# Constant tiles in another order, and what begins at a multiple of 128 bytes

## The chip, the core and the metric

The kernel runs on one core of a Trainium2 chip. The metric is the device time of one execution in microseconds; lower is better. Of several executions the median stands.

## What is computed

Three stages follow each other: a chunked scan with a decay, then a gated layer (SiLU), then a layer with a squared ReLU. All inputs of the layers' weights arrive as 64-bit floats.

```python
def _attn_ref(x, a, B, C):            # x: (4, 8, 768, 32); B, C: (4, 8, 768, 16)
    for c in range(nc):               # chunks of 32 steps
        L = np.exp(cum[:, :, :, None] - cum[:, :, None, :]) * causal
        M = np.einsum('bhin,bhjn->bhij', Cc, Bc) * L
        y[:, :, sl] = M @ xc + np.einsum('bhin,bhnd->bhid', Cc, state) * np.exp(cum)[..., None]
        state = ...                   # decayed state + sum of B x
...
x = attn_out.transpose(0, 2, 1, 3).reshape(3072, 256)
g = x @ w_gate                        # 256 x 1536
x = (g / (1 + np.exp(-g)) * (x @ w_val)) @ w_out      # 1536 x 256
h = np.maximum(x @ w_in, 0)           # 256 x 2048
out = (h * h) @ w_out                 # 2048 x 256
```

## The kernel before

**Stages.** The scan is cut into 28 chunks of 112 (the last of a batch element 96) steps, 7 for each of 4 batch elements. Chunk k has its x in one of three tiles xa, B and C in one of three tiles bc (late chunks) or two tiles eb (early ones), and its decay matrix in one of two tiles mt. Its output goes, transposed, to two large constant tiles: xh_all and xl_all hold the scan's output (and later the gated layer's) as a high and a low part, so that a product of 32-bit numbers is done as three fast matmuls: high by high, high by low, low by high. Weights are turned to 32-bit numbers on the chip (raw, then v) and split into hi and lo, each a tile of 1024 numbers per partition.

**Matmuls.** In the gated layer (function `glu`) the tokens are cut into tiles of 336, 432, 256 and four times 512. For each tile and each of 12 blocks of 128 columns, `front` makes g and v, each from six matmuls (L743) with hi or lo as the stationary and xh_all or xl_all as the moving operand. ACT and DVE make the product t of the two, and from it the tile p with a high and a low half. `back` adds to two accumulators with six matmuls (L857), whose moving operand is p. In the second layer (function `relu2`) six tiles of 512 tokens run over 16 blocks: six matmuls for h (L743), relu on ACT (L909), square on DVE (L912), high half on ACT (L915), low half on DVE (L919), and six matmuls (L929) with p as the moving operand. In the last of the six tiles p is the stationary operand and the matmuls are 256 wide (L938). Order on PE within a six: high weights by high, high weights by low, low weights by high; then the same for the second half.

**Order.** All work is recorded as operations with a cost and a priority, and the class `Graph` plans the order once, from a table of numbers (`PLAN`). The order of instructions on each engine is that of the plan.

**Addresses.** Tiles are laid out in a partition one after another in the order in which they are made, each rounded up to a multiple of 32 bytes: first a few constants, then the tiles of the pool `const`, then the pools w (weights), raw, tmp (t), p, tr, L, ab, xf, st. The tiles of the pools have sizes that are multiples of 128 bytes. So the place where w begins, and with it every later tile, follows from the sum of the sizes of the constant tiles. xh_all and xl_all are the first of them.

Of `const`, two tiles have a size that is no multiple of 128 and not small: delta (1808 bytes in a partition) and dv (3164). spare holds one number, which `act_table` writes to have the table of functions loaded early.

Of the kernel before, what the change touches and what calls it, by code (L numbers as in the profile page):

```python
# [8 lines left out]
F32 = mybir.dt.float32  # L9
F32R = mybir.dt.float32r  # L10
F16 = mybir.dt.float16
BF16 = mybir.dt.bfloat16
# [3 lines left out]
AF = mybir.ActivationFunctionType  # L16
# [117 lines left out]
def kernel(  # L134
# [13 lines left out]
    nc = tc.nc  # L148
    NB, H, S, D = x.shape
# [8 lines left out]
    P = 128  # L158
    G = P // D
    HG = H // G  # L160
    Q = P - NS
# [17 lines left out]
    const = ctx.enter_context(tc.tile_pool(name="const", bufs=1))  # L179
# [8 lines left out]
    NBC, NX, NEB, NMT = 3, 3, 2, 2  # L188
# [6 lines left out]

    xh_all = const.tile([P, 2, T], F32R, name="xh_all")
    xl_all = const.tile([P, 2, T], F32R, name="xl_all")
    delta = const.tile([P, H, Q + 1], BF16, name="delta")
    bc = [const.tile([P, 2, H, NS], F32, name=f"bc{i}") for i in range(NBC)]
    eb = [const.tile([P, 4, P], F32, name=f"eb{i}") for i in range(NEB)]  # L200
    xa = [const.tile([P, H, D], F32, name=f"xa{i}") for i in range(NX)]
    mts = [const.tile([P, H, P], F32, name=f"mt{i}") for i in range(NMT)]
    idle = const.tile([P, 256], BF16, name="idle")
    eye = const.tile([P, P], F32, name="eye")
    pick = const.tile([P, H], F32, name="pick")
    spare = const.tile([1, 1], F32, name="spare")
    dv_all = const.tile([P, NCB, Q + 1], F32, name="dv")
    dv = dv_all[0:R]
    C0 = PLAN["parts"]
# [24 lines left out]

    def act_table():

        nc.scalar.activation(spare, nc.const_aps.tensor(0.0, (1, 1), F32), AF.Silu)


    def zeros():  # L240
# [79 lines left out]
    op_delta = g.add("POOL", 1250, setup_delta, [op_mt], prio=-996)  # L320
    op_bc = g.add("POOL", 2200, setup_bc, prio=-900)
    op_tab = g.add("ACT", 600, act_table, prio=-940)

    def dma(eng, n, cost, move, fn, deps=(), prio=0.0, bufs=(), pieces=256):
# [797 lines left out]
    spare=0,  # L1122
# [107 lines left out]
```

## Time and profile before

| | us |
|---|---|
| median of 3 runs | 642.64 |
| lowest, highest | 641.45, 644.4 |
| the profiled execution | 640.49 |
| its span, first to last instruction | 638.7 |

The span has 9952 instructions. The page gives, for each engine, busy time and its share; a chain of work that ended last; and groups of instructions by line. The names to know: PE does matmuls, PEld loads their stationary operands and overlaps PE, DVE and ACT work on elements, POOL does some of the chunks' steps, SP issues nearly all transfers. A matmul's own duration in the records runs from its start to its modelled end and overlaps with the next one; the distance between two starts is what one costs in a stream. Starts stand in the timeline, in hundredths of a microsecond from the span's start, so a distance is best read over many matmuls. In the timeline equal neighbours are merged into one row with a count.

The run has four parts. Up to some 45 us transfers of weights and chunks set the pace and PE fills gaps with idle matmuls; up to 145 us PE does the chunks and the gated layer for tiles of 336, 432 and 256; up to 362 us the gated layer for tiles of 512, with the small matmuls of 15 chunks in between; then the second layer, the last tile of it from 594 us.

### The profile page before, as it was taken

Reading aid. Unit: us, or ns where it says so; the run is one execution under the profiler, and the core shown is the slowest. Engines: PE = TensorE matmul, PEld = TensorE weight load, DVE = VectorE, ACT = ScalarE, POOL = GpSimd, SP = SyncE. Lnnn points to the kernel's source line nnn. Section 1 sums busy time; section 2 is a strip of 40 time slices with the busy share of each in tenths; the row PEclk is TensorE's granted clock in tenths of the full one; section 3 lists DMA queues with packets and bytes.
Section 4 is the critical chain, followed back from the end, with each engine's and each line's share of the span. In section 5 each row is a group of like instructions: output and inputs, shape, how many; then the busy total and the mean of one; then the engine's idle time right before and its main releaser. Section 6 shows DMA issues by size and latency. Waiting matters only on the chain.

```text
span 638.7 us, 9952 instructions
## 1 busy us (share of the span) xinstructions
PE 631.1 (99%) x3837; PEld 530.0 (83%) x3837; DVE 432.0 (68%) x677; ACT 334.7 (52%) x583; POOL 105.0 (16%) x128
## 2 busy tenths in 40 slices
PE   9899999999999999999999999999999999999997
PEld 7789999998878787877888888888888888888896
DVE  6889897888787878759388855454545554545543
ACT  4888984546434744445366554444444444444442
POOL 4252463223221223114013300000000000000000
PEclk9999999999999999999999999999999999999999
DMA  8979765768656674451023000020010200200201
GB/s 187 212 169 206 207 143 110 126 124 178 114 115 122 162 149 89 73 164 66 1 66 132 1 1 0 1 33 2 5 29 2 33 1 0 34 0 1 34 0 34
DMA packets 155759, 49.92 MB, mean 78 GB/s; under 512 B 143680, under 2 KB 144192, under 8 KB 155712
## 3 DMA queue, kind: packets, MB, share of 16 engines
q1 hardware_dynamic: 155168, 48.93, 35.7%
q8 instruction: 30, 0.49, 0.3%
q10 hardware_dynamic: 544, 0.36, 0.2%
q14 instruction: 17, 0.14, 0.1%
HBM read 34.50 MB, written 3.25 MB: 59 GB/s over the span
## 4 chain that ended last, share of the span: by engine, by line
PE 95%; DMA 2%; SPq 1%; ACT 1%; POOL 0%; issue 0%; DVE 0%; POOLq 0%; ACTq 0%
PE h L743 21%; PE g L743 19%; PE acc L929 17%; PE acc L857 16%; PE v L743 13%; PE acc L938 4%; PE ys L681 2%; PE cb L642 2%; DMA xa<-in_x_dram 1%; DMA raw<-in_moe_w_val_dram 1%; SPq L395 1%; ACT raw L419 0%; PE st L717 0%; SPq L485 0%; PE ab L231 0%; PE cb L634 0%
## 5 line engine op out<-in xcount | busy, mean ns | idle before, releaser
L919 DVE TENSOR_TENSOR p<-t,p 128x512 fp32r<-128x512 f32 x96 | 66.3, 691 | 68.3 <-ACT p L915 68.3
L912 DVE TENSOR_TENSOR t<-t 128x512 f32<-128x512 f32 x96 | 66.5, 693 | 58.3 <-ACT t L909 58.2
L915 ACT ACTIVATE p<-t 128x512 fp32r<-128x512 f32 x96 | 60.7, 633 | 77.8 <-PE acc L929 55.7
L929 PE MATMUL acc<-p,hi 128*128 128x512 f32 x320 | 99.9, 393 | 0.0
L909 ACT ACTIVATE t<-h 128x512 f32<-128x512 f32 x96 | 57.7, 601 | 69.4 <-PE h L743 68.6
L857 PE MATMUL acc<-p,hi 128*128 128x512 f32 (+5 forms) x328 | 91.2, 363 | 0.0
L807 ACT ACTIVATE t<-g 128x512 f32<-128x512 f32 (+6 forms) x90 | 45.6, 512 | 67.4 <-PE g L743 52.5
L830 DVE TENSOR_TENSOR p<-t,p 128x512 fp32r<-128x512 f32 (+5 forms) x82 | 64.3, 801 | 17.4 <-ACT p L825 16.8
L743 PE MATMUL h<-xh_all,hi 128*128 128x512 f32 x192 | 75.8, 395 | 0.0
L743 PE MATMUL h<-xl_all,hi 128*128 128x512 f32 x192 | 75.3, 392 | 0.0
L743 PE MATMUL h<-xh_all,lo 128*128 128x512 f32 x192 | 75.3, 392 | 0.0
L929 PEld LDWEIGHTS acc<-p,hi 128*128 128x128 f32 x320 | 60.1, 188 | 13.5
L743 PE MATMUL g<-xh_all,hi 128*128 128x512 f32 (+5 forms) x196 | 69.0, 352 | 0.0
L825 ACT ACTIVATE p<-t 128x512 fp32r<-128x512 f32 (+5 forms) x82 | 45.2, 560 | 43.0 <-DVE t L810 25.0
L743 PE MATMUL g<-xh_all,lo 128*128 128x512 f32 (+5 forms) x196 | 67.5, 344 | 0.0
L743 PE MATMUL g<-xl_all,hi 128*128 128x512 f32 (+5 forms) x196 | 67.3, 343 | 0.0
L857 PEld LDWEIGHTS acc<-p,hi 128*128 128x128 f32 x328 | 58.0, 189 | 7.6
L810 DVE TENSOR_TENSOR t<-t,v 128x512 f32<-128x512 f32 (+2 forms) x66 | 42.5, 646 | 30.9 <-PE v L743 27.7
L929 PE MATMUL acc<-p,lo 128*128 128x512 f32 x160 | 63.2, 395 | 0.0
L857 PE MATMUL acc<-p,lo 128*128 128x512 f32 (+5 forms) x164 | 58.8, 359 | 0.0
L743 PE MATMUL v<-xh_all,hi 128*128 128x512 f32 (+2 forms) x132 | 50.4, 382 | 0.0
L743 PE MATMUL v<-xh_all,lo 128*128 128x512 f32 (+2 forms) x132 | 49.7, 377 | 0.0
(97 smaller groups left out, 1085.7 us busy)
## 6 DMA issues: line engine op xcount, KB each, us to landing
ab<-decay SPq DMA_DIRECT2D x22, 452.0 KB, 4.1
raw<-in_moe_w_out_dram SPq DMA_DIRECT2D x14, 512.0 KB, 5.1
raw<-in_moe_w_in_dram SPq DMA_DIRECT2D x8, 512.0 KB, 4.0
raw<-in_moe_w_gate_dram SPq DMA_DIRECT2D x6, 512.0 KB, 5.9
raw<-in_moe_w_val_dram SPq DMA_DIRECT2D x6, 512.0 KB, 4.8
xa<-in_x_dram SPq DMA_DIRECT2D x24, 112.0 KB, 2.8
out_dram<-o SPq DMA_DIRECT2D x40, 64.0 KB, 2.0
bc<-in_B_dram SPq DMA_DIRECT2D x18, 56.0 KB, 2.8
```

The lines of the kernel that those rows point to most:

```text
L743: nc.tensor.matmul(ps, l, r, start=(i == 0), stop=(i == len(terms) - 1))
L807: nc.scalar.activation(t[:, :n], gg(), AF.Silu)
L810: nc.vector.tensor_tensor(tb.t[:, :n], tb.t[:, :n], vv(), op=ALU.mult)
L825: nc.scalar.activation(p[:, 0, :n], tb.t[:, :n], AF.Copy)
L830: e.tensor_tensor(p[:, 1, :n], tb.t[:, :n], p[:, 0, :n].bitcast(F32), op=ALU.subtract)
L857: nc.tensor.matmul(ps, l, r, start=bank not in done_f, stop=f == NF - 1, skip_group_check=True,)
L909: nc.scalar.activation(new(tb, [P, TN], F32, "t"), ph.t, AF.Relu)
L912: nc.vector.tensor_tensor(tb.t, tb.t, tb.t, op=ALU.mult)
L915: nc.scalar.activation(new(pb, [P, 2, TN], F32R, "p")[:, 0, :], tb.t, AF.Copy)
L919: e.tensor_tensor(pb.t[:, 1, :], tb.t, pb.t[:, 0, :].bitcast(F32), op=ALU.subtract)
L929: nc.tensor.matmul(acc[-1 - i][m], l.t[:, w], pb.t[:, r, :], start=(f == 0 and s == 0), stop=(f == NF2 - 1 and s == 2),)
L938: nc.tensor.matmul(acc[-1 - i][q][:, :256], pb.t[:, l, tk], r, start=(f == 0 and s == 0), stop=(f == NF2 - 1 and s == 2),)
```

## The change

The tiles of `const` are made in another order: xa and mt right behind xl_all, then bc, eb, idle, eye, and only then delta. spare becomes 24 numbers long, and the instruction that writes it is given its first number.

```diff
     xh_all = const.tile([P, 2, T], F32R, name="xh_all")
     xl_all = const.tile([P, 2, T], F32R, name="xl_all")
-    delta = const.tile([P, H, Q + 1], BF16, name="delta")
+    xa = [const.tile([P, H, D], F32, name=f"xa{i}") for i in range(NX)]
+    mts = [const.tile([P, H, P], F32, name=f"mt{i}") for i in range(NMT)]
     bc = [const.tile([P, 2, H, NS], F32, name=f"bc{i}") for i in range(NBC)]
     eb = [const.tile([P, 4, P], F32, name=f"eb{i}") for i in range(NEB)]
-    xa = [const.tile([P, H, D], F32, name=f"xa{i}") for i in range(NX)]
-    mts = [const.tile([P, H, P], F32, name=f"mt{i}") for i in range(NMT)]
     idle = const.tile([P, 256], BF16, name="idle")
     eye = const.tile([P, P], F32, name="eye")
+    delta = const.tile([P, H, Q + 1], BF16, name="delta")
     pick = const.tile([P, H], F32, name="pick")
-    spare = const.tile([1, 1], F32, name="spare")
+    spare = const.tile([1, 24], F32, name="spare")
...
-        nc.scalar.activation(spare, nc.const_aps.tensor(0.0, (1, 1), F32), AF.Silu)
+        nc.scalar.activation(spare[:, 0:1], nc.const_aps.tensor(0.0, (1, 1), F32), AF.Silu)
```

The built programs have the same instructions in the same order on all five engines, with the same waits. What differs is where tiles begin in a partition:

| tiles | first byte before | remainder by 128 | first byte after | remainder by 128 |
|---|---|---|---|---|
| xh_all, xl_all | 1152, 25728 | 0 | 1152, 25728 | 0 |
| delta | 50304 | 0 | 69760 | 0 |
| xa0 to xa2 | 59296, 60320, 61344 | 32 | 50304, 51328, 52352 | 0 |
| mt0, mt1 | 62368, 66464 | 32 | 53376, 57472 | 0 |
| bc0 to bc2 | 52128, 53152, 54176 | 32 | 61568, 62592, 63616 | 0 |
| eb0, eb1 | 55200, 57248 | 32 | 64640, 66688 | 0 |
| idle, eye | 70560, 71072 | 32 | 68736, 69248 | 0 |
| pick, spare | 71584, 71616 | 32, 64 | 71584, 71616 | 32, 64 |
| dv | 71648 | 96 | 71712 | 32 |
| weights (v, hi, lo), 20 slots of 4096 | 74816 on | 64 | 74880 on | 0 |
| raw, t, p and all later pools | 156736, 173120, 181312 on | 64 | 64 bytes further | 0 |

A stationary operand is 512 bytes of such a slot, beginning at a multiple of 512 in it. A 512-wide moving operand is 2048 bytes, beginning at a multiple of 2048 in xh_all, xl_all or p. The tiles of 432 and 336 tokens are rows of 1728 and 1344 bytes, which are 13.5 and 10.5 times 128; the moving operand of the tile of 432 begins 1344 bytes into xh_all, at a remainder of 64.

## Rows read from the trace of the kernel before

**Rows 1.** The page: engines (busy us, share, instructions), and the chain that ended last.

```profile
PE 631.1 (99%) x3837; PEld 530.0 (83%) x3837; DVE 432.0 (68%) x677; ACT 334.7 (52%) x583; POOL 105.0 (16%) x128
...
PE 95%; DMA 2%; SPq 1%; ACT 1%; POOL 0%; issue 0%; DVE 0%; POOLq 0%; ACTq 0%
```

**Rows 2.** Busy time by stage: stage, length, engines' busy us, granted clock, DMA share, GB/s.

```profile
145.00:362.00 217.00, 217.00 (x1254) 174.53 (x1253) 166.77 (x247) 112.46 (x200) 52.98 (x59) 1.00 0.46 104
362.00:594.00 232.00, 232.00 (x1006) 188.54 (x1005) 123.06 (x181) 104.50 (x170) 0.00 (x0) 1.00 0.06 10
```

**Rows 3.** Groups by shape: line, operation, count, busy us, mean ns, idle us before.

```profile
L929 PE MATMUL acc<-p,hi 128*128 128x512 f32 x320 | 99.9, 393 | 0.0
L743 PE MATMUL h<-xh_all,hi 128*128 128x512 f32 x192 | 75.8, 395 | 0.0
...
L857 PE MATMUL acc<-p,hi 128*128 128x512 f32 x192 | 60.5, 396 | 0.0
...
L743 PE MATMUL g<-xh_all,hi 128*128 128x512 f32 x96 | 38.1, 396 | 0.0
```

**Rows 4.** Timeline of PE, second layer: start, length, line, operation, count.

```profile
418.67 0.40 PE L743 MATMUL h<-xh_all,hi 128*128 128x512 f32 x1
...
420.06 0.63 PE L929 MATMUL acc<-p,hi 128*128 128x512 f32 x2
...
426.99 0.40 PE L743 MATMUL h<-xh_all,hi 128*128 128x512 f32 x1
```

**Rows 5.** Timeline of PE, a long run of v and g.

```profile
351.58 0.39 PE L743 MATMUL v<-xh_all,hi 128*128 128x512 f32 x1
...
360.51 0.63 PE L857 MATMUL acc<-p,hi 128*128 128x512 f32 x2
```

**Rows 6.** Timeline of PE, 24 matmuls with p, and the h behind them.

```profile
364.66 0.63 PE L857 MATMUL acc<-p,hi 128*128 128x512 f32 x2
...
367.43 0.61 PE L857 MATMUL acc<-p,hi 128*128 128x512 f32 x2
...
370.15 0.40 PE L743 MATMUL h<-xh_all,hi 128*128 128x512 f32 x1
```

**Rows 7.** Timeline of PE, first layer, from one p to the next.

```profile
301.12 0.63 PE L857 MATMUL acc<-p,hi 128*128 128x512 f32 x2
...
305.27 0.63 PE L857 MATMUL acc<-p,hi 128*128 128x512 f32 x2
```

**Rows 8.** Timeline of PE, a run of g and v behind 256-wide matmuls.

```profile
160.06 0.40 PE L743 MATMUL g<-xl_all,hi 128*128 128x512 f32 x1
...
166.59 0.39 PE L743 MATMUL g<-xh_all,lo 128*128 128x512 f32 x1
```

**Rows 9.** Timeline of PE, 256-wide: with p, then with xh_all and xl_all.

```profile
158.39 0.40 PE L857 MATMUL acc<-p,hi 128*128 128x256 f32 x2
...
159.83 0.40 PE L743 MATMUL g<-xh_all,hi 128*128 128x512 f32 x1
...
139.22 0.28 PE L743 MATMUL g<-xh_all,hi 128*128 128x256 f32 x1
...
143.46 0.41 PE L857 MATMUL acc<-p,hi 128*128 128x256 f32 x2
```

**Rows 10.** Timeline of PE, 432-wide.

```profile
94.66 0.36 PE L743 MATMUL g<-xh_all,hi 128*128 128x432 f32 x1
...
99.16 0.36 PE L743 MATMUL v<-xh_all,lo 128*128 128x432 f32 x1
```

**Rows 11.** Waits of PE, longest in total: us, times, longest.

```profile
PE g L743 <- ACT xf L696: 1.2, 1, 1.2
```

**Rows 12.** The chain that ended last, its two longest pieces at the start.

```profile
7.56 5.46 DMA raw<-in_moe_w_val_dram
...
22.96 6.11 DMA xa<-in_x_dram
```

## The prediction

> **What bounds the kernel now.** I read the shares of the page first: PE is busy for 99% of the span, and the chain of work that ended last is 95% PE [rows 1]. Then the busy time by stage: from 145 us to 594 us PE has no idle time at all, at a granted clock of 1.00, which is 2.4 GHz [rows 2]. Nothing there waits for DVE, ACT, POOL or a transfer; the longest wait of PE in the whole run is 1.2 us [rows 11]. So the time is the number of matmuls times the distance between their starts. The columns "busy" and "mean ns" don't give that distance, because matmuls overlap (a 512-wide one shows 393 ns [rows 3]); the starts in the timeline do.
>
> The matmuls 512 columns wide carry the run. By shape they are 480 on L929 (320 with hi, 160 with lo), 576 for h (three groups of 192), 288 on L857 (192 and 96) and 576 for g and v (six groups of 96) [rows 3]: 1920 in all. In the second layer's steps 36 of them take 426.99 - 418.67 = 8.32 us, so 231.1 ns each [rows 4]. 512 columns at 2.4 GHz are 213.3 ns.
>
> Now the rows that matter. Two kinds of matmul have the same shape, the same engine and weights from the same slots, and differ in where the moving operand lies: xh_all and xl_all begin at a multiple of 128 bytes, p at 64 past one; the weights (hi, lo) are always at 64 past one. In long runs of one kind they settle at two rates. A run on xh_all and xl_all goes from 351.58 to 360.51 us, 39 matmuls: 229.0 ns each [rows 5]. A run of 24 on p needs 2.77 us for its first 12, 230.8 ns each, and 2.72 us for its last 12: 226.7 ns each [rows 6]. Neither rate is reached in the second layer, where the kind changes after every six: there the mean is 231.1 ns [rows 4], worse than both. In the first layer a step of six on p and twelve on xh_all and xl_all takes 305.27 - 301.12 = 4.15 us for 18, or 230.5 ns [rows 7]. I read this as two costs: 2.3 ns per matmul where weights and moving operand have a different remainder by 128, and some 25 ns each time that the remainder of the moving operand changes, spread over the next ten matmuls.
>
> **The change, part by part.** No instruction is added, removed or moved: on all five engines the same instructions stand in the same order, and the planner, its pools and its costs see nothing of it. Only addresses differ. After it weights, p, xh_all and xl_all all begin at a multiple of 128 bytes. So the state that the p run shows, weights and moving operand with one remainder, holds for every 512-wide matmul, and the remainder of the moving operand doesn't change any more. I take 226.7 ns, the rate of that row.
>
> - Second layer, five tiles of 16 steps of 12: 960 x (231.1 - 226.7) = 4.2 us saved [rows 4, 6].
> - First layer, 48 steps of 18: 864 x (230.5 - 226.7) = 3.3 us at the rate of [rows 7]. From this two things go off. Steps made of longer runs are nearer to 229.0 already [rows 5], which I set at 0.4 us. And after each of the 15 chunks whose small matmuls come between them here, the first 512-wide ones need some 25 ns to settle, as the first 12 of the p run do ((230.8 - 226.7) x 12 = 49 ns at most [rows 6]); that stays: 15 x 25 ns = 0.4 us. Left: 2.5 us.
> - Last tile of the second layer, 96 matmuls on xh_all and xl_all between 256-wide ones: at most 96 x 4.4 ns = 0.4 us; I take 0.2, because every six follow a change of width.
> - 256-wide matmuls speak the other way: on xh_all (other remainder than the weights) they start every 4.24 us / 36 = 117.8 ns, on p (same remainder) every 1.44 us / 12 = 120.0 ns [rows 9]. If that too goes by the remainder, the 144 on xh_all and xl_all lose 2.2 ns each: 0.3 us lost. Bounds: 0.3 us lost to, if p goes the other way, 0.2 us gained. I take 0.3 lost.
> - 432-wide ones on xh_all have the weights' remainder already and stand at 4.50 us / 23 = 195.7 ns [rows 10], while 17/16 of a column's time, the rate of the p run, would be 191.3. Their rows are 13.5 times 128 bytes long, so the remainder changes within each. I take nothing for them and for the 336-wide ones, with 0.5 us either way: some 320 of them at 1.6 ns.
> - Loads into xa, bc and eb begin at a multiple of 128 in place of 32 past one. They are on the chain only in the start, where the two longest pieces are 5.46 us and 6.11 us [rows 12]. No row shows the same load at another remainder. I take nothing, because the bytes and packets stay; a twentieth of these two pieces is 0.6 us either way.
> - DVE, ACT and POOL get other addresses as well; PE has no wait for them from 145 us on [rows 2, 11], so what they gain or lose in a step of 2.77 us is hidden up to the point where they fill it.
>
> Sum: 4.2 + 2.5 + 0.2 - 0.3 = 6.6 us. The profiled execution took 640.5 us (span 638.7), which would become 633.9. The median of the three runs is 642.64, 2.1 us above it; the saving is made in stages that are PE alone, so I take it off the median: **636.0 us**.
>
> **Rivals.**
>
> *Nothing happens.* Then 229.0 against 226.7 comes from something else than the remainder (another tile, two tiles read in turn instead of one), and the time stays at 642.6. For it: the 256-wide and 432-wide rows show no gain from equal remainders [rows 9, 10]. Against: the cost at every change of kind [rows 4], though weight slots all over the memory give the same rate. The Trainium skill speaks for this rival: its page "TensorE: Matmul & The Clock Gate", section "Step-by-step: what each phase is for", gives PE two independent read ports, one for the moving operand and one for the weights, so that loading weights takes nothing from a running matmul; by that rule addresses relative to each other would not matter and the time would be 642.6. The trace here doesn't agree fully, since two kinds of one shape differ by 2.3 ns; why, no row shows.
>
> *Only the changes go.* The rate of 229.0 belongs to moving operands at a multiple of 128, whatever the weights do. Then p comes to 229.0 too, and only the settling goes: 960 x 2.1 + 864 x 1.5 less 0.4 = 2.9 us, so 639.7 us. Against it: nothing makes an operand at 64 past a line better than one on it, unless the weights count.
>
> *A worse state holds.* One run on xh_all and xl_all didn't settle at 229.0: from 160.06 to 166.59 us, 28 matmuls, each takes 233.2 ns [rows 8]. It began after 256-wide matmuls and kept its rate to the end, so there is more than one stable state, and which one is entered depends on what ran ahead. If with equal remainders no change ever throws PE out of a bad state, the whole run may sit in it: 960 x 2.1 + 864 x 2.7 + 0.3 = 4.7 us lost, 647.3 us. It decides from the point where more than (230.8 - 226.7) / (233.2 - 226.7), about six in ten, of the 512-wide matmuls are in it (230.8 being the mean of both layers). Against it: the p run left its first, slower matmuls by itself [rows 6].
>
> **How the numbers follow.** A measurement of this kernel tells about 0.5% (3.2 us) from no change. Chances: the forecast 0.60; only the changes go 0.10, half of it beyond 0.5%; nothing 0.19; the worse state 0.11. That gives faster 0.65, same 0.24, slower 0.11. The forecast by itself spans 634.2 (no settling left, the other widths and the loads for the better) to 638.0. The range for 8 in 10 takes in the second rival and most of the first, and at its low end half a microsecond for the spread of the runs: 633.6 to 643.3.
>
> **What would show it.** In the second layer a step from one h to the next goes from 2.77 us to 2.72 us, and the stretch that was 362 to 594 us gets about 4 us shorter; the long run of v and g takes 226.7 ns per matmul in place of 229.0, the end of the p run stays at 226.7. PE stays without idle time. If the p run moves to 229.0, the remainder of the moving operand alone counts; if the step stays at 2.77 us, it isn't the remainder; if runs stand at 233 ns, the worse state is there. The forecast is wrong if the last 12 of the p run owed their rate to something other than the address, for instance to p being one tile.

## The result, and the profile after

| | before | after |
|---|---|---|
| median, us | 642.8 | 634.85 |
| lowest to highest, us | 641.45 to 644.4 | 633.99 to 636.27 |
| the profiled execution, us | 640.49 | 633.99 |
| its span, us | 638.7 | 632.2 |

Four runs of each. The ratio of after to before is 0.9878, with a 95% interval of 0.9848 to 0.9907. The forecast was 636.0 us, in a range of 633.6 to 643.3. The profiled span fell by 6.5 us, where the sum said 6.6.

The page of the changed kernel, engines and chain, as in [rows 1]: PE is still the bound, with 6.2 us less busy time for the same 3837 matmuls. (This chain can be followed back to 66.48 us only; that is why its shares add up to 89% and PE has 88% in place of 95%.)

```profile
PE 624.9 (99%) x3837; PEld 530.2 (84%) x3837; DVE 431.9 (68%) x677; ACT 334.3 (53%) x583; POOL 104.9 (17%) x128
...
PE 88%; DVE 1%; issue 0%
```

The stages of the changed kernel, as in [rows 2] (length, busy us and count of PE, PEld, DVE, ACT, POOL, granted clock, DMA share, GB/s). PE has no idle time, at the same granted clock of 1.00 (2.4 GHz). In the same 232 us it gets through 1037 matmuls instead of 1006 (some of the 31 more are 256-wide, because the last tile begins earlier).

```profile
145.00:362.00 217.00, 217.00 (x1267) 176.56 (x1266) 168.13 (x249) 113.53 (x203) 52.51 (x59) 1.00 0.46 105
362.00:594.00 232.00, 232.00 (x1037) 192.61 (x1036) 125.16 (x184) 106.15 (x173) 0.00 (x0) 1.00 0.07 12
```

The timeline of PE (start, length, line, operation, count), second layer, as in [rows 4]: three steps of twelve from one h to the next take 426.91 - 418.75 = 8.16 us, which is 226.7 ns per matmul, before 231.1.

```profile
418.75 0.39 PE L743 MATMUL h<-xh_all,hi 128*128 128x512 f32 x1
...
426.91 0.39 PE L743 MATMUL h<-xh_all,hi 128*128 128x512 f32 x1
```

The same view, a long run on xh_all and xl_all as in [rows 5], and the 24 matmuls on p as in [rows 6]. The first is 358.91 - 350.07 = 8.84 us for 39, so 226.7 ns in place of 229.0. The second takes 2.72 us for its first twelve and 2.72 us for its last twelve. The slower start of 2.77 us is gone.

```profile
350.07 0.39 PE L743 MATMUL v<-xh_all,hi 128*128 128x512 f32 x1
...
358.91 0.62 PE L857 MATMUL acc<-p,hi 128*128 128x512 f32 x2
...
362.99 0.62 PE L857 MATMUL acc<-p,hi 128*128 128x512 f32 x2
...
365.71 0.62 PE L857 MATMUL acc<-p,hi 128*128 128x512 f32 x2
...
368.43 0.39 PE L743 MATMUL h<-xh_all,hi 128*128 128x512 f32 x1
```

A step of the first layer, as in [rows 7]: 4.08 us for 18, 226.7 ns, before 4.15 us, 230.6 ns (the prediction has it as 230.5).

```profile
300.43 0.62 PE L857 MATMUL acc<-p,hi 128*128 128x512 f32 x2
...
304.51 0.62 PE L857 MATMUL acc<-p,hi 128*128 128x512 f32 x2
```

The run behind 256-wide matmuls which stood at 233.2 ns [rows 8]: now 167.11 - 160.50 = 6.61 us for 29, or 227.9 ns. Its first five are slower (234, 236, 228, 232 and 231 ns from start to start, 28 ns more in sum than five at 226.7); then it stays at 226.7. So after another width PE still has to settle, but here it does so, to 226.7, where before it stayed at 233.2 to the end of the run.

```profile
160.50 0.40 PE L743 MATMUL g<-xh_all,hi 128*128 128x512 f32 x1
...
167.11 0.39 PE L743 MATMUL g<-xh_all,lo 128*128 128x512 f32 x1
```

The 256-wide ones on xh_all and xl_all, as in [rows 9]: 42 in 5.05 us, 120.2 ns, before 117.8. That is the loss that the sum had.

```profile
139.10 0.28 PE L743 MATMUL g<-xh_all,hi 128*128 128x256 f32 x1
...
144.15 0.40 PE L857 MATMUL acc<-p,hi 128*128 128x256 f32 x2
```

Where the 6.5 us went, by the starts of the same matmuls in both traces:

| stretch | before, us | after, us | saved | forecast |
|---|---|---|---|---|
| to the first 336-wide matmul | 45.83 | 45.54 | 0.29 | 0 |
| from there to the first 256-wide | 77.23 | 77.97 | -0.74 | 0 |
| from there to the first 512-wide | 27.98 | 28.24 | -0.26 | -0.3 |
| first 512-wide to the first h | 210.86 | 208.51 | 2.35 | 2.5 |
| first h to the first L938 | 232.88 | 228.48 | 4.40 | 4.2 |
| from there to the last 512-wide | 33.61 | 33.61 | 0.00 | 0.2 |
| from there to the end of the span | 10.31 | 9.84 | 0.47 | 0 |

Of the second line's loss 0.45 us is one wait of PE on DVE at 70.94 us, the only one between 44 and 146 us in the changed kernel (idle time and its releaser stand at the end of the row); in the kernel before PE has none there. The rest of that line is not located.

```profile
70.94 0.97 PE L857 MATMUL acc<-t,v 128*128 128x208 f32 x4 [0.45 <-DVE t L810]
```

### The profile page after: what moved, and what is told of

The parts are those of the page before. It is cut to its first block, busy times and chain, and to the rows that moved or that the text cites. A ratio compares the mean times of both kernels' runs of the same rounds, so it can differ in the third digit from the quotient of the medians.

```text
span 632.2 us, 9952 instructions
## 1 busy us (share of the span) xinstructions
PE 624.9 (99%) x3837; PEld 530.2 (84%) x3837; DVE 431.9 (68%) x677; ACT 334.3 (53%) x583; POOL 104.9 (17%) x128
## 4 chain that ended last, share of the span: by engine, by line
PE 88%; DVE 1%; issue 0%
PE h L743 21%; PE acc L929 17%; PE g L743 16%; PE acc L857 15%; PE v L743 13%; PE acc L938 4%; PE ys L681 2%; PE cb L642 2%; DVE L L606 1%; DVE mt L667 0%; DVE o L985 0%; DVE t L810 0%
## 5 line engine op out<-in xcount | busy, mean ns | idle before, releaser
L929 PE MATMUL acc<-p,hi 128*128 128x512 f32 x320 | 98.4, 389 | 0.0
L830 DVE TENSOR_TENSOR p<-t,p 128x512 fp32r<-128x512 f32 (+5 forms) x82 | 62.5, 780 | 17.2 <-ACT p L825 16.7
L743 PE MATMUL v<-xl_all,hi 128*128 128x512 f32 (+2 forms) x132 | 49.4, 374 | 0.0
```

The costliest lines, as they stand in the source:

```text
L743: nc.tensor.matmul(ps, l, r, start=(i == 0), stop=(i == len(terms) - 1))
L830: e.tensor_tensor(p[:, 1, :n], tb.t[:, :n], p[:, 0, :n].bitcast(F32), op=ALU.subtract)
L929: nc.tensor.matmul(acc[-1 - i][m], l.t[:, w], pb.t[:, r, :], start=(f == 0 and s == 0), stop=(f == NF2 - 1 and s == 2),)
```

## The experiments

All of them compute everything and change addresses alone, by the length of spare or by a small tile that nothing reads, laid out ahead of others. Below, "distance" is the first byte of the weights minus the first byte of the moving operand. In the kernel before it was -64 bytes for xh_all and xl_all and 0 for p; after the change it is 0 for both. The names of the two theories that were left after the result:

- *Same place*: operands must begin at multiples of 128 bytes (the words of the change), or at one remainder by 128 (the words of the prediction).
- *Distance*: only weights minus moving operand counts, with a period and a sign of its own.

A clean measure beside the median is the time from the start of the first 512-wide matmul to the start of the last one, since in the stretch ahead of it the profiled executions differ by up to 7 us (first 512-wide at 150.5 to 157.8 us) with no pattern by address. It stands in the table for every kernel. For e4_p_off and e5_w_off the distances in the table hold for the first layer alone; in the second layer part of the weights lie in other pools, at other distances.

| kernel | distance to xh_all, xl_all | distance to p | first to last 512-wide, us | median, us | ratio to before, 95% interval |
|---|---|---|---|---|---|
| before | -64 | 0 | 477.35 | 642.8 | |
| after | 0 | 0 | 470.61 | 634.85 | 0.9848 to 0.9907 |
| e1_all64 | 0 | 0 | 470.61 | 633.97 | 0.9841 to 0.9885 |
| e2_spare_only | 0 | 0 | 470.76 | 636.46 | 0.9895 to 0.9948 |
| e3_order_only | -64 | 0 | 477.35 | 641.53 | 0.9989 to 1.0024 |
| e8_x64 | -64 | 0 | 477.35 | 642.93 | 0.9994 to 1.0049 |
| e12_plus192 | +192 | 0 | 477.35 | 642.11 | 0.9988 to 1.0025 |
| e9_plus256 | +256 | 0 | 470.61 | 634.47 | 0.9866 to 0.9931 |
| e6_plus128 | +128 | 0 | 478.02 | 642.03 | 0.9983 to 1.0021 |
| e7_rel32 | +32 | 0 | 480.26 | 645.1 | 1.0038 to 1.0088 |
| e11_minus32 | -32 | 0 | 480.50 | 645.24 | 1.0043 to 1.0084 |
| e10_w_only | -64 | -64 | 474.25 | 638.44 | 0.9935 to 0.9977 |
| e4_p_off | 0 | -64 | 477.51 | 641.24 | 0.9967 to 1.0009 |
| e5_w_off | +64 | -64 | 478.10 | 641.73 | 0.9980 to 1.0013 |

The ratios are to runs of the kernel before beside each (medians 641.47 to 641.94 us for the experiments).

### Which part of the change: e2_spare_only, e3_order_only

The order of before with the longer spare, and the order of after with the short one.

```diff
 # e2_spare_only, against before
-    spare = const.tile([1, 1], F32, name="spare")
+    spare = const.tile([1, 24], F32, name="spare")
...
-        nc.scalar.activation(spare, nc.const_aps.tensor(0.0, (1, 1), F32), AF.Silu)
+        nc.scalar.activation(spare[:, 0:1], nc.const_aps.tensor(0.0, (1, 1), F32), AF.Silu)
```

```diff
 # e3_order_only, against after
-    spare = const.tile([1, 24], F32, name="spare")
+    spare = const.tile([1, 1], F32, name="spare")
```

> The kernel before with spare 24 numbers long and nothing else: weights and p at multiples of 128, the tiles of the chunks (xa, mt, bc, eb) still 32 past one. If the gain is all in the 512-wide matmuls: time within 0.3% of the changed kernel, 633 to 637 us, second-layer step 2.72 us. If the order of the chunks' tiles carries some of it: the time of the first 151 us is longer than in the changed kernel by that part, and the whole lies between 637 and 642 us.

> The changed kernel with spare one number long again: the tiles of the chunks at multiples of 128, weights and p 64 past one. If the gain is all in the 512-wide matmuls: as the kernel before, 641 to 644.5 us, second-layer step 2.77 us. If the chunks' tiles carry some of it: shorter by that part, in the first 151 us.

The order by itself gives nothing (1.0006), and its long stretch is that of before to the last digit. The spare tile by itself gives the long stretch of after, within 0.15 us. In e2_spare_only a long run on xh_all and xl_all takes 365.12 - 356.28 = 8.84 us for 39, as after the change:

```profile
356.28 0.39 PE L743 MATMUL v<-xh_all,hi 128*128 128x512 f32 x1
...
365.12 0.62 PE L857 MATMUL acc<-p,hi 128*128 128x512 f32 x2
```

Its median of 636.46 is 1.6 us above that of after. The two intervals overlap; its interval doesn't reach that of e1_all64, which has the new order and ends at 0.9885. What differs in its profiled execution lies ahead of the long stretch: it begins 6 us later. The stages of e2_spare_only show where: between 30 and 50 us the granted clock is 0.74, a mean of time at both levels, behind a stage in which PE was busy for 13.49 of 15 us. The changed kernel has a clock of 1.00 in the same 20 us and a short dip ahead of it. Less work of PE ahead doesn't explain it: in e3_order_only PE was busy for 13.07 us of the same 15, and the clock stayed at 1.00 from 30 to 50 us. Why it fell more here, no run shows. The stages of e2_spare_only, then of the changed kernel:

```profile
15.00:30.00 15.00, 13.49 (x217) 11.21 (x215) 13.69 (x28) 12.05 (x20) 3.63 (x4) 1.00 0.83 187
30.00:50.00 20.00, 17.64 (x196) 13.91 (x196) 12.22 (x21) 13.52 (x21) 7.47 (x6) 0.74 0.64 134
```

```profile
15.00:30.00 15.00, 14.69 (x233) 11.97 (x222) 12.76 (x26) 12.39 (x21) 4.50 (x4) 0.91 0.93 212
30.00:50.00 20.00, 18.91 (x208) 16.90 (x209) 16.95 (x26) 17.90 (x28) 9.11 (x9) 1.00 0.83 175
```

The ten runs of e2_spare_only lie at 634.29 to 640.52 us, so the start varies from run to run. Whether the order of the chunk tiles has a share of a microsecond or two in how the start goes, stays open. What the change gains from the first 512-wide matmul on doesn't come from it: 6.59 of the 6.74 us are there with the old order.

### Absolute place or distance: e1_all64, e8_x64

Everything from xh_all on moves by 64 bytes (e1_all64), or xh_all, xl_all and the chunk tiles alone do, with a shorter spare that leaves weights and p where after has them (e8_x64).

```diff
 # e1_all64, against after
+    const.tile([1, 16], F32, name="pad")
     xh_all = const.tile([P, 2, T], F32R, name="xh_all")
```

```diff
 # e8_x64, against after
+    const.tile([1, 16], F32, name="pad")
     xh_all = const.tile([P, 2, T], F32R, name="xh_all")
...
-    spare = const.tile([1, 24], F32, name="spare")
+    spare = const.tile([1, 8], F32, name="spare")
```

> The changed kernel with 64 unused bytes ahead of xh_all, so that xh_all, xl_all, weights and p all begin 64 past a multiple of 128. If only equal remainders count (my theory): 226.7 ns per 512-wide matmul everywhere, second-layer step 2.72 us, time within 0.3% of the changed kernel, 633 to 637 us. If a begin at a multiple of 128 counts by itself: 229 ns or more per matmul, 639 us or more.

> The kernel before turned round: xh_all and xl_all 64 past a multiple of 128, weights and p at multiples of 128. My theory: as the kernel before, 226.7 ns in long runs on p, 229.0 ns in long runs on xh_all and xl_all, step 2.77 us, 641 to 644.5 us. If a begin at a multiple of 128 counts by itself: p's matmuls as in the changed kernel and only those on xh_all and xl_all dearer, step 2.74 to 2.75 us, 637 to 640 us.

In e1_all64 xh_all, xl_all, weights and p all begin 64 past a multiple of 128, and it is as fast as after: the whole gain is there. In e8_x64 weights and p do begin at multiples of 128 and only xh_all and xl_all at 64 past one, and nothing is left of the gain. So the words of the change, multiples of 128, name no cause. The timeline, a long run on xh_all and xl_all in e1_all64 (8.84 us for 39, 226.7 ns), then the same in e8_x64 (8.92 us, 228.7 ns):

```profile
351.63 0.39 PE L744 MATMUL v<-xh_all,hi 128*128 128x512 f32 x1
...
360.47 0.62 PE L858 MATMUL acc<-p,hi 128*128 128x512 f32 x2
```

```profile
353.20 0.39 PE L744 MATMUL v<-xh_all,hi 128*128 128x512 f32 x1
...
362.12 0.63 PE L858 MATMUL acc<-p,hi 128*128 128x512 f32 x2
```

### Which distances are equal: e6_plus128, e9_plus256, e12_plus192

Only the length of spare differs from after, and with it the place of weights, p and all later pools.

```diff
-    spare = const.tile([1, 24], F32, name="spare")
+    spare = const.tile([1, 56], F32, name="spare")   # e6_plus128
+    spare = const.tile([1, 88], F32, name="spare")   # e9_plus256
+    spare = const.tile([1, 72], F32, name="spare")   # e12_plus192
```

> The changed kernel with weights, p and all later pools moved on by 128 bytes: remainders by 128 stay equal, those by 256 and more differ between xh_all and the weights. If 128 is the length that counts: 226.7 ns everywhere, 633 to 637 us. If it is 256 or more: as in the kernel before, step 2.77 us, 641 to 644 us.

> spare is 88 numbers long, so that weights, t, p and all later pools begin 256 bytes further on than in the changed kernel; xh_all and xl_all stay. Weights then stand 256 bytes past the remainder of xh_all by 512, and at its remainder by 256. Theory (the offset between weights and moving operand counts, by 256): every 512-wide run takes 226.7 ns per matmul and the median is 634 to 636.5 us. Rival 1 (it counts by 512 or a longer stretch): runs on xh_all and xl_all take 229 to 233.5 ns while those on p settle at 226.7, and the median is 641 to 645.5 us. Rival 2 (an offset is good only where it is exactly nought by 512 and cheap where small): a rate between 227 and 229 on xh_all, 637 to 641 us.

> spare is 72 numbers long, so that weights, p and all later pools begin 192 bytes further on than in the changed kernel: weights 192 bytes above the remainder of xh_all and xl_all, p at the remainder of the weights. Theory (only the remainder by 256 of the distance counts, sign and all): 192 above is the same as 64 below, so long runs on xh_all and xl_all take 229.1 ns per matmul, the six-matmul runs of the second layer settle anew at each change, from the first 512-wide matmul to the last it is 477.4 us as in the kernel before, and the median is 640.5 to 643 us. Rival (nought and 256 are good, and every distance above costs alike, as 32, 64 and 128 do): 233 ns on xh_all and xl_all, 478 us or more from first to last, and 642 to 645.5 us.

At +128 every operand of a 512-wide matmul begins at a multiple of 128, so that all remainders by 128 are nought, yet the gain is gone and the long run on xh_all and xl_all is worse than before: 9.10 us for 39, 233.3 ns. The p run of the same kernel, at distance 0, still ends at 2.72 us for twelve. At +256 everything is as after. At +192 everything is as before, where the distance is -64, to the last digit of the long stretch. So the period is 256, not 128: 256 above is as nought, and 192 above is 64 below. The rows, in this order: long run and last half of the p run in e6_plus128, then the long run in e9_plus256 (8.84 us), then in e12_plus192 (8.92 us).

```profile
352.46 0.39 PE L743 MATMUL v<-xh_all,hi 128*128 128x512 f32 x1
...
361.56 0.63 PE L857 MATMUL acc<-p,hi 128*128 128x512 f32 x2
...
368.46 0.62 PE L857 MATMUL acc<-p,hi 128*128 128x512 f32 x2
...
371.18 0.40 PE L743 MATMUL h<-xh_all,hi 128*128 128x512 f32 x1
```

```profile
349.94 0.39 PE L743 MATMUL v<-xh_all,hi 128*128 128x512 f32 x1
...
358.78 0.62 PE L857 MATMUL acc<-p,hi 128*128 128x512 f32 x2
```

```profile
351.95 0.39 PE L743 MATMUL v<-xh_all,hi 128*128 128x512 f32 x1
...
360.87 0.63 PE L857 MATMUL acc<-p,hi 128*128 128x512 f32 x2
```

### Small distances: e7_rel32, e11_minus32

```diff
-    spare = const.tile([1, 24], F32, name="spare")
+    spare = const.tile([1, 32], F32, name="spare")   # e7_rel32
+    spare = const.tile([1, 16], F32, name="spare")   # e11_minus32
```

> The changed kernel with weights, p and later pools 32 bytes further on: 32 past a multiple of 128, xh_all and xl_all at one. The trace doesn't say what a difference of 32 costs. If any difference costs the same: second-layer step 2.77 us, 641 to 644 us. If the cost grows with the difference up to 64: half of it, 638 to 640 us. If 32 and 96 are worse than 64, over 645 us.

> spare is 16 numbers long, so that weights, p and all later pools begin 32 bytes ahead of where the changed kernel has them: weights 32 bytes below the remainder of xh_all and xl_all, p at the remainder of the weights. Theory (the cost grows with the distance on this side): long runs on xh_all take about 227.9 ns, half way from 226.7 to 229.1, and the median is 637 to 641 us. Rival 1 (any offset below the moving operand's costs the same): 229.1 ns and 641 to 643.5 us, as 64 bytes below. Rival 2 (a distance of 32 costs as much on either side): 233 ns and 643.5 to 646 us, as 32 bytes above.

Both are slower than before, by 0.6%: the two kernels at 32 bytes, either way, are the slowest of all. The cost doesn't grow with the distance, which was my theory for e11_minus32; its second rival came true. Long runs take 9.11 us for 39 in e7_rel32 and 9.10 us in e11_minus32, 233.6 and 233.3 ns; a difference of 0.01 us is the last digit of these starts, so the two rates are not told apart.

```profile
356.22 0.40 PE L743 MATMUL v<-xh_all,hi 128*128 128x512 f32 x1
...
365.33 0.63 PE L857 MATMUL acc<-p,hi 128*128 128x512 f32 x2
```

```profile
354.72 0.40 PE L743 MATMUL v<-xh_all,hi 128*128 128x512 f32 x1
...
363.82 0.63 PE L857 MATMUL acc<-p,hi 128*128 128x512 f32 x2
```

### Cost per matmul and cost per change: e10_w_only, e4_p_off, e5_w_off

The prediction had two costs: one for every matmul at a distance, one for every change of it. In e10_w_only p is laid out last, behind a tile of 64 bytes, and spare has one number: all moving operands are at -64 from the weights, and there is no change. In e4_p_off p alone is moved. In e5_w_off tiles of 64 bytes stand ahead of w, p and tr.

```diff
 # e10_w_only, against after; the pools' tiles are made in the order of this list
-    for k, v in pools.items()
+    for k in ["w", "raw", "tmp", "tr", "L", "ab", "xf", "st", "p", "ps"]:
+        if k == "p":
+            pad = ctx.enter_context(tc.tile_pool(name="pad", bufs=1))
+            pad.tile([1, 16], F32, name="pad")
...
-    spare = const.tile([1, 24], F32, name="spare")
+    spare = const.tile([1, 1], F32, name="spare")
```

```diff
 # e4_p_off (k in p, tr) and e5_w_off (k in w, p, tr), against after
+        if k in {'p': 64, 'tr': 64}:
+            pad = ctx.enter_context(tc.tile_pool(name="pad_" + k, bufs=1))
+            pad.tile([1, 16], F32, name="pad_" + k)
```

> spare is one number long again, and the pool p is laid out last, behind a tile of 64 bytes. So weights stand 64 bytes below the remainder of xh_all and xl_all, as before the change, but p has the remainder of xh_all: the weights differ from every moving operand by the same 64 bytes, and the moving operand's remainder never changes. Theory (a cost per matmul by the offset, and one per change of it): no settling at the changes between h and p, all 512-wide matmuls at 229.0 to 229.2 ns, a step of the second layer at 2.75 us, median 638 to 640 us. Rival 1 (the settling belongs to any change of the moving tile unless the offset is nought): the second layer's step stays at 2.77 us or more and the median is 641 to 643.5 us. Rival 2 (p alone decides, xh_all and xl_all having 226.7 or 229.1 by what p did): the step at 2.72 us and 634 to 636.5 us.

> The changed kernel with a pad ahead of the pool p and one behind it, so that p alone begins 64 past a multiple of 128; weights, xh_all and xl_all stay at multiples of 128. My theory: long runs on xh_all and xl_all at 226.7 ns, long runs on p at 229.0 ns, and some 25 ns at each change of kind: second-layer step 2.76 to 2.78 us, 640 to 643 us. If p at 64 is the better place by itself: 635 us or less.

> The changed kernel with pads between the pools, so that weights begin 64 past a multiple of 128, while xh_all, xl_all and p stay at multiples of 128. My theory of two costs (2.3 ns per matmul where weights and moving operand differ, and a cost where the moving operand's remainder changes): the first is paid by all 1920, the second by none: 229.0 ns everywhere, second-layer step 2.75 us, 1920 x 2.3 ns = 4.4 us more than the changed kernel, 638.5 to 640 us. If only the changes cost: 635 us, as the changed kernel. If each difference costs as in the kernel before: 642 to 644 us.

e10_w_only came out as the theory of two costs said. Its steps of the second layer take 425.65 - 417.41 = 8.24 us for 36, so 228.9 ns for p, xh_all and xl_all alike, with nothing added at a change:

```profile
417.41 0.39 PE L746 MATMUL h<-xh_all,hi 128*128 128x512 f32 x1
...
425.65 0.39 PE L746 MATMUL h<-xh_all,hi 128*128 128x512 f32 x1
```

That splits the cost. Of the 6.74 us that after saves from the first to the last 512-wide matmul (477.35 - 470.61), e10_w_only keeps 3.10 although its 768 matmuls on p are dearer by 2.2 ns (1.7 us); 0.16 of it is in the last tile. So the changes in the kernel before cost about 3.10 - 0.16 + 1.7 = 4.6 us. In the second layer this is, per change, half of 12 x 231.1 - 6 x 228.9 - 6 x 226.7 = 39.6 ns: some 20 ns.

Both costs belong to the distance -64 and not to any distance. At +128 the long runs are dearer (233.3 ns), but three steps of the second layer take 425.15 - 416.85 = 8.30 us, 230.6 ns per matmul, and before 231.1. The same sum gives 12 x 230.6 - 6 x 233.3 - 6 x 226.7 = 7 ns for two changes, some 4 ns each. So a long run alone doesn't tell what a kernel that alternates will take. From e6_plus128:

```profile
416.85 0.40 PE L743 MATMUL h<-xh_all,hi 128*128 128x512 f32 x1
...
425.15 0.40 PE L743 MATMUL h<-xh_all,hi 128*128 128x512 f32 x1
```

In e4_p_off the roles are turned round (p at -64, xh_all and xl_all at 0). Its second layer isn't clean, since the pools behind p move by 128 bytes and by then hold part of the weights; the first layer is. From the first 512-wide matmul to the first h it takes 364.57 - 154.17 = 210.40 us, near the 210.86 of before and not the 208.51 of after. So the cost goes with the distance and not with the tile. The p run, still on weights of the first layer, takes 5.51 us for 24, 229.6 ns; in the kernel before p settled at 226.7.

```profile
367.37 0.63 PE L859 MATMUL acc<-p,hi 128*128 128x512 f32 x2
...
372.88 0.39 PE L745 MATMUL h<-xh_all,hi 128*128 128x512 f32 x1
```

e5_w_off isn't the kernel that its expectation speaks of: the tiles of 64 bytes add up, so that p stands 128 bytes and not nought from xh_all, and the later pools 192. It can't be read as weights alone being off; e10_w_only is the kernel for that. It still gives a distance of its own: +64 for xh_all and xl_all. There a long run takes 9.10 us for 39, 233.3 ns, where -64 gives 228.7 to 229.0. So the sign counts.

```profile
353.81 0.39 PE L745 MATMUL v<-xh_all,hi 128*128 128x512 f32 x1
...
362.91 0.62 PE L859 MATMUL acc<-p,hi 128*128 128x512 f32 x2
```

## Why the prediction was right, and where it was not

**The rate.** That the state of the p run, 226.7 ns, would hold for every 512-wide matmul came true in the second layer, between first h and first L938: 228.48 us / 226.67 ns are 1008 matmuls, and 1008 stand there. The forecast counted 960 of them here; the other 48 are the last ones on p of the first layer and the first h of the last tile, and they are the 0.2 us that this stretch gave beyond its term. Shown, by the kernels at distance 0 and 256 (after, e1_all64, e2_spare_only, e9_plus256).

**What the remainder is by.** This step of the prediction failed, and the change's own words with it. One remainder by 128 is not enough: e6_plus128 has it and no gain. Multiples of 128 aren't needed: e1_all64 has the gain without them. It is the distance between weights and moving operand, by 256. The forecast came true because this change makes the distance 0, and that is right under either rule. That was luck: with spare 56 numbers long in place of 24 the prediction's words would have been the same, and the gain nothing (e6_plus128). The rows of before couldn't tell: only the distances -64 and 0 occur in them for this shape.

**Two costs.** Both exist (e10_w_only). The one per matmul was sized at 2.3 ns and is 2.2 (228.9 - 226.7). The one per change was sized at 25 ns and is some 20. Neither is one number; both go by the distance: in long runs a matmul costs 2.2 ns more at -64, and some 6.6 at +32, -32, +64 and +128; a change costs some 20 ns at -64 and some 4 at +128.

**First layer, 2.5 forecast, 2.35 found.** The settling behind other widths does stay, as the term said; the slower first five matmuls of the run at 160.50 us are an example.

**Last tile, 0.2 forecast, nothing found.** The stretch takes 33.61 us in both. Each six there follows 256-wide matmuls, and that change of width costs as much at distance 0 as before. In the chain that ended last, of the changed kernel (start, length, what, count), such a six takes 1.39 us, some 232 ns per matmul:

```profile
604.44 1.39 PE h L743 x6
```

**256-wide, 0.3 lost forecast, 0.26 found.** The one term that speaks against the change was read rightly from [rows 9].

**432- and 336-wide, nothing forecast.** From the first 432-wide to the first 256-wide matmul it is 51.19 us before and 51.21 after, and the run of [rows 10] still takes 99.67 - 95.17 = 4.50 us for 23, 195.7 ns. The prediction says that they have the weights' remainder; by 256 they don't. Their operand begins 64 past xh_all, so their distance was 128 before and is -64 after, 0 in neither, and they were no sign for *Nothing happens*. Nor is 0 their best: the same run takes 100.64 - 96.15 = 4.49 us in e5_w_off, where their distance is 0, and in e6_plus128, where it is +64, 23 of them take 105.91 - 101.46 = 4.45 us, 193.5 ns, with the later ones at 193.3.

```profile
101.46 0.36 PE L743 MATMUL g<-xh_all,hi 128*128 128x432 f32 x1
...
105.91 0.36 PE L743 MATMUL v<-xh_all,lo 128*128 128x432 f32 x1
```

The reason given, 17/16 of a column's time, doesn't stand: at distance 0 three widths take 120.0, 153.4 and 226.7 ns, which at 2.4 GHz are 288, 368 and 544 columns for 256, 336 and 512 (means of the distances within runs in the changed kernel). That is 32 more in each case, not a sixteenth; it is arithmetic, and no run was made for it. The 193.3 ns of the 432-wide ones at +64 are 464 columns, 32 more as well; at distance 0 they don't reach it.

**Start and loads, nothing forecast, 0.6 either way.** Up to the first 256-wide matmul 0.29 us were saved in one stretch and 0.74 lost in the next in these two executions, 0.45 lost in sum. Across all the kernels it moves by up to 7 us, so nothing of it is put down to the change.

**The rivals.** *Nothing happens* is out by the result: by the distance, long runs take 226.7 to 233.6 ns. The rule of the Trainium skill that stood for it (page "TensorE: Matmul & The Clock Gate", section "Step-by-step: what each phase is for": two independent read ports, loading weights takes no read bandwidth from the running matmul) would make all distances equal. The traces here don't agree with that; whether the ports are where it fails, no run shows. *Only the changes go* is out, since xh_all and xl_all went to 226.7. *A worse state holds* is out for this change. Its rate is no accident of one run, though: the run behind 256-wide matmuls takes 233 ns in e3_order_only, e8_x64 and e12_plus192 as well, and the long runs of e7_rel32 and e11_minus32 have that rate throughout; whether it is the same state, no run shows. Had spare been 32 numbers long in place of 24, the same change would have been 0.6% slower than before.

The predicted median was 1.15 us above the measured one. The profile's sum was right within 0.1 us; the rest is where the profiled execution of before lay, 2.1 us below the median that the sum was taken off, while that of after lay 0.9 us below its own.

## What to carry to other kernels

When PE has no idle time, measure the distance between starts in runs that differ in one thing, and print the first byte of both operands beside it: some 1% lay in the length of a tile that holds one number (6.59 us of the long stretch of e2_spare_only). For 512-wide matmuls like these, lay out weights and moving operands so that their first bytes differ by a multiple of 256 (other widths had other best distances here), and don't take "aligned to 128" as enough. A small constant tile can move every later pool, so after any edit of constants look again at where the large tiles begin, since 32 bytes the wrong way made this kernel 0.6% slower than before the change.

## What the runs showed that I had not expected

The distance between weights and moving operand governs the rate of 512-wide matmuls, with a period of 256 bytes and a sign (runs of 39, as above):

| distance by 256 | 0 | 32 | 64 | 128 | 192 | 224 |
|---|---|---|---|---|---|---|
| ns per matmul, long runs | 226.7 | 233.6 | 233.3 | 233.3 | 228.7 to 229.0 | 233.3 |

What in the chip does this no run shows, and 96 and 160 were not tried. Nor does the distance settle the rate by itself. At 192 (that is -64) the run behind 256-wide matmuls stands at 233.2 ns in the kernel before [rows 8], while in e10_w_only, with the same distance to xh_all and xl_all and p at it too, the same run takes 166.43 - 159.78 = 6.65 us for 29, 229.3 ns. So what ran ahead counts as well, except at 0, where every long run settled at 226.7.

```profile
159.78 0.40 PE L746 MATMUL g<-xh_all,hi 128*128 128x512 f32 x1
...
166.43 0.40 PE L746 MATMUL g<-xh_all,lo 128*128 128x512 f32 x1
```

The best distance isn't the same for all widths. In e5_w_off, at +64, where the 512-wide ones are slow, the 256-wide ones on xh_all and xl_all take 136.33 - 130.32 = 6.01 us for 53, or 113.4 ns, the fastest seen; after has 120.2 and before 117.8.

```profile
130.32 0.28 PE L745 MATMUL g<-xh_all,hi 128*128 128x256 f32 x1
...
136.33 0.28 PE L745 MATMUL g<-xh_all,lo 128*128 128x256 f32 x1
```

But the next run of the same kernel, at the same distance, takes 144.60 - 139.65 = 4.95 us for 42, or 117.9 ns, so this rate too isn't fixed by the distance alone:

```profile
139.65 0.28 PE L745 MATMUL g<-xh_all,hi 128*128 128x256 f32 x1
...
144.60 0.40 PE L859 MATMUL acc<-p,hi 128*128 128x256 f32 x2
```

For the 144 of them that would be at most 144 x 6.8 ns = 1.0 us, as an estimate, if their part of xh_all and xl_all alone stood 64 bytes off and all of them ran at 113.4. That wasn't tried; it is under what a measurement of this kernel can tell.
